# Regrouping transfers on two queues and a later third pair of scores in a fused attention and MLP kernel on one Trainium2 core

## The chip, the cores and the metric

The kernel runs on one core of a Trainium2 chip. The metric is the device time of one execution in microseconds; lower is better. All times here are of one core.

## The reference

What is computed is a layer norm, then multi-query attention (one key and value head for 16 query heads) and an MLP on the normed input, and the sum of all three:

```python
B, S, D, H = 1, 2048, 448, 16          # Dh = 28, F = 1792
def _A_ref(x, wq, wk, wv, wo):
    q = (x @ wq).reshape(B, S, H, Dh).transpose(0, 2, 1, 3)
    k = x @ wk
    v = x @ wv
    scores = jnp.einsum("bhqd,bkd->bhqk", q, k) * (Dh ** -0.5)
    p = _softmax(scores, axis=-1)
    o = jnp.einsum("bhqk,bkd->bhqd", p, v)
    return o.transpose(0, 2, 1, 3).reshape(B, S, H * Dh) @ wo
def _B_ref(x, w1, b1, w2, b2):
    y = _layernorm(x, axis=-1)
    h = _gelu(jnp.einsum("bsd,df->bsf", y, w1) + b1)
    return jnp.einsum("bsf,fd->bsd", h, w2) + b2
xn = _layernorm(x, axis=-1)
return x + _A_ref(xn, A_wq, A_wk, A_wv, A_wo) + _B_ref(xn, B_w1, B_b1, B_w2, B_b2)
```

All data is float32.

## The kernel before

The order of all instructions on each engine is written out by hand; the framework adds the semaphores. The program has three stages: norm and projections (to about 120 us), the MLP with part of the row maxima of the scores beside it (to about 490 us), and attention, in which the change lies.

**Units and steps.** The 2048 queries are cut into 4 chunks of 512, the 16 heads into 4 groups of 4; a unit `u` is one chunk and one group, 16 units in all. The 2048 keys are 16 tiles of 128, and a step treats two key tiles of one unit, so a unit has 8 steps (`kt` = 0, 2, ... 14), and there are 128 steps. The loop at the end of `block_kernel` walks through a string of letters for each step, `ORDERS[0]` for units 0 and 1 and `ORDERS[1]` for units 2 to 15 (`TURNED`), and each letter issues one piece of work:

- `p`: `scores`, a pair of matmuls (L776) that make two heads' or tiles' scores in one of two PSUM buffers, keys in partitions, and one exponential of both on ScalarE (L778). In units 2 to 15 only three of the four heads are made this way, so a step has three pairs.
- `t`, `x`, `T`: the fourth head of units 2 to 15. Its scores are made with queries in partitions (`turned_scores`, `t`, L735), VectorE scales them into a tile `raw` in SBUF and takes the row maximum (L736); four `t` fill one tile of 128 queries, and a unit has four such tiles. `turned_exp` (`x`) makes the exponential of half a tile on ScalarE (L753) and issues eight transfers from SBUF to SBUF (L756), each of 32 partitions by 512 numbers, 64 KB, that regroup the 32-row blocks into the tile `turned` of the unit. `turn_blocks` (`T`) then transposes 32 by 32 blocks of `turned` on VectorE (L761), for two key tiles at a time, so that the keys lie in partitions as for the other heads. The first `T` of a unit needs all 64 transfers of the unit. The work for unit `u` runs ahead, during the unit before; `x` takes one waiting half tile each time, and a second one in the step `kt` = 12. There are three `raw` and two `turned` buffers.
- `P`: the burst, `BURST` = 2 times `pv`: eight matmuls (L715) that multiply the exponentials of the step before with the values and add to the unit's sum `po`. The profile counts 16 matmuls, two passes each.
- `m`: one matmul (L475) and one reduction (L476) of the row maxima for later units, if the plan (`weight`) is behind.
- `e`: `load_max`, once a unit, turns the maxima on TensorE (L458) and sends them into the `q` tile of the next unit.
- `n`: one piece of `norm_jobs`, which divides a finished unit's sum by its softmax denominator; it issues the small transfers `rc`, `ld`, `tr` (L656 to L664) and runs three operations on GpSimd (L667 to L674).
- `o`: one piece of the output projection: for one tile of 128 queries twelve matmuls (L629 to L631), an addition, a transfer to the result.

PSUM banks for `t`, `m`, `e` and `o` come from a pool of three (`mtile`). In the attention stage all loads of `q` (`load_q`, `load_m`) are issued by GpSimd, the 64 transfers a unit of `turned_exp` by SyncE. Each engine and each queue works in the order of its program.

**Output weights.** They are loaded into one of the two `turned` buffers and split there into a high and a low part by `prep_wo`: ScalarE copies (L612) and GpSimd subtracts (L613), four groups, all in step 12.

Of the kernel before, what the change touches and what calls it, by code (L numbers as in the profile page):

```python
# [10 lines left out]
AF = mybir.ActivationFunctionType  # L11
# [7 lines left out]
CT = 4  # L19
NCH = NT // CT  # L20
CW = CT * P
NG = H // 4
# [2 lines left out]
SCALE = DH ** -0.5  # L25
BURST = 2
MLP_MAX = 20
ORDERS = ("mptmpmtmpmexnPTpmonm", "tptmpmeopxnPTmnm")
TURNED = tuple(range(2, 16))
RAWS = 3  # L30
LEAD = 11
# [5 lines left out]
def block_kernel(ctx, tc, x, wq, wk, wv, wo, w1, b1, w2, b2, out):  # L37
    nc = tc.nc
    pe, act, dve, pool = nc.tensor, nc.scalar, nc.vector, nc.gpsimd
    ctx.enter_context(tc.manual_schedule())  # L40

    def f(t):
        return t.bitcast(F32)
# [50 lines left out]
    def mtile(shape):  # L94
        return mp.tile(shape, F32, name="m")
# [95 lines left out]
    def bn_end(c, k0=0, n=CT):  # L191
        for k in range(k0, k0 + n):
            dve.bn_aggr(lnp[:, CT * c + k, :], sts[c][:, k, :])
        ts = slice(CT * c + k0, CT * c + k0 + n)
        r = rstd(lnr[:, ts], lnp[:, ts, 1], n)
        next(r)
        yield
        next(r)
        dve.scalar_tensor_tensor(lnb[:, ts], lnp[:, ts, 0], -1.0, lnr[:, ts], op0=ALU.mult, op1=ALU.mult)
        yield  # L200
# [9 lines left out]
    def norm_both():  # L210
        dve.tensor_mul(lnq, lnp[:, :, 1], lnr)
        dve.tensor_mul(lnq, lnq, lnr)
        r = rstd(lnq, lnq, NT)
        next(r)
        yield
        next(r)
        dve.tensor_mul(lnq, lnq, lnr)
        dve.scalar_tensor_tensor(lnqb, lnp[:, :, 0], -1.0, lnq, op0=ALU.mult, op1=ALU.mult)
        act.activation(warm, one, AF.Gelu_apprx_tanh)
        yield  # L220
# [54 lines left out]
    def norm_gen(c, bank):  # L275
        center, turn = norm_parts(c, True, False, bank)
        for k in range(CT + 1):
            if k < CT:
                center(k)
            if k > 0:  # L280
                turn(k - 1)
            yield
# [88 lines left out]
    for c, at in ((2, ((0, 1), (0, 2), (0, 2), (0, 3))), (3, ((1, 0), (1, 1), (1, 2), (1, 3)))):  # L371
        for k in range(CT):
            later(*at[k], lambda t=CT * c + k: bn(t))
        g = bn_end(c)
        for k in range(2):
            later(c - 1, 0, lambda g=g: next(g), True)
    g = norm_both()
# [28 lines left out]
    for c in range(NCH):  # L406
        center, turn = norm_parts((c + 1) % NCH, c + 1 == NCH)
        for i in range(4):
# [7 lines left out]
            if i in ((2, 3) if c == 0 else (1, 3)):  # L416
                n = 2 * c + i // 3
# [19 lines left out]
    def load_q(u):  # L437
        c, g = units[u]
        cols = slice(c * CW, (c + 1) * CW)
        if u < 2:  # L440
            qst.append(xt_p.tile([P, 4, CW], F32R, name="xh"))
            pool.memset(f(qst[u]), 0.0)
        qs = qst[u % 2]
        for blk, i in ((1, 0), (2, 0), (0, 1), (3, 1)):
            nh = heads_of(u)
            src = qd[i][4 * DH * g:4 * DH * g + DH * nh, cols].rearrange("(j r) n -> r j n", r=DH)
            loads.dma_start(f(qs[32 * blk:32 * blk + DH, 0:nh, :]), src)
        qss[u] = qs
# [50 lines left out]
    mxs, side, oside = Stream(), Stream(), Stream()  # L499
# [63 lines left out]
    for c in range(1, NCH):  # L563
        g = norm_gen(c, lambda shape: php.tile(shape, F32, name="ph"))
# [4 lines left out]
    for n in range(len(mslots) + 2):  # L569
        c, ft = mslots[n] if n < len(mslots) else (NCH, n - len(mslots))  # L570
        if ft == 12:
            for k in range(CT):
                a = acc[:, CT * c + k, :]
# [20 lines left out]
    def turned_tile():  # L594
        return att.tile([P, 4 * CT, CW], F32, name="turned", bufs=2)

    wor = turned_tile()[:, 0:NG, 0:D]
# [5 lines left out]
    woh = att.tile([P, NG, D], F32R, name="woh", bufs=1)  # L603
    wol = att.tile([P, NG, D], F32R, name="wol", bufs=1)
# [2 lines left out]
        src = wo.rearrange("(g j d) n -> j d g n", j=4, d=DH)[j]  # L607
        nc.sync.dma_start(wor[32 * j + 1:32 * j + 1 + DH, :, :], src)

    def prep_wo():  # L610
        for g in range(NG):
            act.activation(woh[:, g, :], wor[:, g, :], AF.Copy)  # L612
            pool.tensor_sub(wol[:, g, :], wor[:, g, :], f(woh[:, g, :]))  # L613

    rows = {}

    def load_rows_of(c, tiles):
        for k in tiles:
            rows[c, k] = att.tile([P, D], F32, name="a", bufs=5)
            loads.dma_start(rows[c, k], ad[:, CT * c + k, :])  # L620

    def o_jobs(c, gs, tiles=range(CT)):
        last = NG - 1 in gs
        for k in tiles:
            po = mtile([P, D])
            ts = slice(k * P, (k + 1) * P)
            for g in gs:
                oth, otl = ots[c, g]
                pe.matmul(po, oth[:, ts], woh[:, g, :], start=(g == gs[0]), stop=False)  # L629
                pe.matmul(po, oth[:, ts], wol[:, g, :], start=False, stop=False)  # L630
                pe.matmul(po, otl[:, ts], woh[:, g, :], start=False, stop=(g == gs[-1]))  # L631
            a = rows[c, k]
            dve.tensor_add(a, a, po)
            if last:
                (nc.scalar if k % 2 and c == NCH - 1 else nc.sync).dma_start(ov[:, CT * c + k, :], a)
            yield
# [73 lines left out]
    def pv(u, kt):  # L710
        if kt == 0:
            pos[u] = op.tile([P, CW], F32, name="po")
        po = pos[u]
        for j in range(4):
            pe.matmul(po[32 * j:32 * j + 32, :], vs[:, kt, :], ps.pop((u, kt, j)),  # L715
                      start=(kt == 0), stop=(kt == NT - 1))
        if kt == NT - 1:
            if u == NU - 1:
                end_jobs(u, pos.pop(u))
                return  # L720
            side.add(norm_jobs(u, pos.pop(u)))
            side.step()
            c, g = units[u]
            if c < NCH - 1 and g == NG - 1:
                oside.add(o_wait(c, range(NG), range(CT if c < NCH - 2 else 2)))

    turned, exps = {}, []

# [17 lines left out]
    def turned_exp():  # L746
        if not exps:
            return
        u, t, raw, m3, h = exps.pop(0)
        if u not in turned:  # L750
            turned[u] = turned_tile()
        rs = slice(2 * h, 2 * h + 2)
        act.activation(raw[:, rs], raw[:, rs], AF.Exp, bias=m3[:, 4:5], scale=1.0)  # L753
        for r in range(2 * h, 2 * h + 2):
            for a in range(4):
                nc.sync.dma_start(turned[u][32 * r:32 * r + 32, 4 * t + a, :],  # L756
                                  raw[32 * a:32 * a + 32, r].rearrange("p b i -> p (b i)"))

    def turn_blocks(u, kt):
        p = pair_of()  # L760
# [11 lines left out]
    def scores(u, kt, jobs):  # L772
        s = sp.tile([P, 2, CW], F32, name="s")
        p = pair_of()
        for i, (k, j) in enumerate(jobs):
            pe.matmul(s[:, i], ks[:, (kt + k) * P:(kt + k + 1) * P], qss[u][:, j, :], start=True, stop=True)  # L776
            ps[u, kt + k, j] = p[:, i]
        act.activation(p, s, AF.Exp, scale=SCALE)  # L778

    def o_wait(c, gs, tiles):  # L780
        load_rows_of(c, tiles)
        for _ in range(8):
            yield
        yield from o_jobs(c, gs, tiles)

    steps = [(u, kt) for u in range(NU) for kt in range(0, NT, 2)]
# [2 lines left out]
    left = total - maxed  # L789
    weight = [0 if n >= len(steps) - LEAD else 24 if u == 0 else 20 if u == 1 else 6 for n, (u, kt) in enumerate(steps)]  # L790
    for n, (u, kt) in enumerate(steps):
        if n == 12:
            prep_wo()
        if u + 1 < NU and kt == 0:
            load_q(u + 1)
        jobs = [((0, 0), (0, 1)), ((0, 2), (1, 2)), ((1, 0), (1, 1))]
        if u not in TURNED:
            jobs[1:2] = [((0, 2), (0, 3)), ((1, 2), (1, 3))]
        for what in ORDERS[u in TURNED]:
            if what == "p":  # L800
                scores(u, kt, jobs.pop(0))
            elif what == "m":
                if maxed < total - left + left * sum(weight[:n + 1]) / sum(weight):
                    maxed += mxs.step()
            elif what == "t":
                if n >= 8 * (TURNED[0] - 1) - 2:
                    tq.step()
            elif what == "x":
                turned_exp()
                if kt == 12:  # L810
                    turned_exp()
            elif what == "T":
                if u in TURNED:
                    turn_blocks(u, kt)
            elif what == "e":
                if kt == (6 if u + 2 < NU else 10) and u + 1 < NU:
                    load_max(u + 1)
            elif what == "n":
                side.step()
            elif what == "o":  # L820
                if n == len(steps) - LEAD:
                    load_rows_of(NCH - 2, (2, 3))
                    for k in (2, 3):
                        for gs in ((0, 1), (2, 3)):
                            oside.add(o_jobs(NCH - 2, gs, [k]))
                elif n == len(steps) - 5:
                    oside.add(o_jobs(NCH - 1, range(NG - 1)))
                if n == len(steps) - 7:
                    load_rows_of(NCH - 1, range(CT))
                oside.step()  # L830
            elif what == "P":
                for _ in range(BURST if n else 0):
                    pv(*pvq.pop(0))
    while pvq:
        pv(*pvq.pop(0))
# [27 lines left out]
```

## Time and profile before

| | us |
|---|---|
| median of 3 runs | 1213.79 (1213.04 to 1216.76) |
| profiled execution | 1212.41 |
| its span on the core | 1210.4 |
| TensorE busy | 1137.7 |
| VectorE busy | 907.4 |
| ScalarE busy | 660.8 |
| GpSimd busy | 353.6 |

The profile is of one execution. The busy times are shares of the span: an engine that is 94% busy over the whole can still wait in one stage, and matmuls are pipelined, so that a busy TensorE is not one at its peak. Instructions that only issue a transfer are not counted as busy on SyncE; the time that SyncE's queue spends on them is read from the order of time. In the rows, PE is TensorE (PEld its weight loads), DVE VectorE, ACT ScalarE, POOL GpSimd, SP SyncE, "SPq" its queue; `out<-in` names the tiles; `L715` is line 715 of the kernel; "idle before <-releaser" is how long the engine stood still ahead of an instruction and what ended it. In the chain and the timeline the first number is the start in us from the span's start, the second the duration.

### The profile page before, as it was taken

How to read it: one execution, taken by the hardware profiler on the slowest of the kernel's cores; microseconds unless marked ns; L12 is line 12 of the kernel's file. 1: busy time of each engine (PE TensorE's matmuls, PEld its weight loads, DVE VectorE, ACT ScalarE, POOL GpSimd, SP SyncE). 2: the span in 40 equal slices, each digit the busy share in tenths (PEclk: the TensorE clock that was granted, in tenths of full speed). 3: DMA queues.
4: the chain of work that ended last, by engine and by line, in shares of the span. 5: the costliest groups of instructions: out<-in, count | busy, mean ns of one | idle time of the engine just before them, and what ended most of it. 6: DMA issues, size and time to landing. Idle time of an engine off the chain costs nothing.

```text
span 1210.4 us, 17322 instructions
## 1 busy us (share of the span) xinstructions
PE 1137.7 (94%) x5793; PEld 722.4 (60%) x5793; DVE 907.4 (75%) x1678; ACT 660.8 (55%) x778; POOL 353.6 (29%) x473
## 2 busy tenths in 40 slices
PE   9999999999999999899989889989889989889998
PEld 8778888888888888544434345334345434344444
DVE  7799999999999999677767566667656767657634
ACT  5842321221221112578877666777766768668763
POOL 5333331131122123525243332143232233223310
PEclk9999999999999999999999899999989989899999
DMA  8651101001000120424554654554654555555520
GB/s 282 198 166 52 35 20 54 16 24 46 24 16 23 47 54 17 119 62 107 126 142 120 156 146 127 123 144 123 161 137 120 132 135 132 132 131 132 130 86 31
DMA packets 77733, 121.86 MB, mean 101 GB/s; under 512 B 24862, under 2 KB 33756, under 8 KB 77516
## 3 DMA queue, kind: packets, MB, share of 16 engines
q1 hardware_dynamic: 64204, 95.63, 29.2%
q0 software_dynamic: 12032, 24.55, 8.1%
q8 instruction: 46, 0.75, 0.3%
q10 hardware_dynamic: 1408, 0.57, 0.2%
q14 instruction: 43, 0.35, 0.1%
HBM read 46.11 MB, written 14.79 MB: 50 GB/s over the span
## 4 chain that ended last, share of the span: by engine, by line
PE 74%; DVE 7%; ACT 7%; DMA 6%; SPq 3%; issue 2%; POOL 0%; ACTq 0%; DVEq 0%; POOLq 0%
PE po L715 16%; PE m L475 14%; PE s L776 12%; PE ph L159 9%; ACT p L778 6%; DMA turned<-raw 5%; PE m L735 4%; PE m L532 3%; PE m L534 3%; PE m L530 3%; SPq L756 3%; DVE mx L476 2%; PE qp L159 2%; DVE p L761 2%; PE m L629 1%
## 5 line engine op out<-in xcount | busy, mean ns | idle before, releaser
L476 DVE TENSOR_REDUCE mx<-m 128x1 f32<-128x512 f32 x800 | 521.4, 686 | 52.1 <-PE m L475 46.8
L778 ACT ACTIVATE p<-s 128x1024 f32<-128x1024 f32 x400 | 387.7, 1022 | 202.0 <-PE s L776 188.8
L475 PE MATMUL m<-ks,qm 128*128 128x512 f32 x800 | 320.5, 404 | 42.4 <-DVE raw L736 41.1
L776 PE MATMUL s<-xh,ks 128*128 128x512 f32 x800 | 265.9, 416 | 19.2 <-ACT p L778 17.8
L761 DVE STREAM_TRANSPOSE p<-turned 128x1024 f32<-128x1024 f32 x112 | 139.4, 1245 | 170.5 <-ACT p L778 72.7
L715 PE MATMUL po<-p,vs 128*32 128x512 f32 x2048 | 258.1, 618 | 1.1 <-DVE p L761 1.1
L516 ACT ACTIVATE hr<-ph,b1t 128x512 f32<-128x512 f32 x56 | 38.6, 688 | 305.4 <-PE ph L164 299.5
L475 PEld LDWEIGHTS m<-ks,qm 128*128 128x128 f32 x800 | 151.6, 190 | 84.1 <-DVE raw L736 46.3
L776 PEld LDWEIGHTS s<-xh,ks 128*128 128x128 f32 x800 | 143.0, 191 | 98.4 <-ACT p L778 64.8
L521 POOL TENSOR_TENSOR hl<-hr,hh 128x512 fp32r<-128x512 f32 x56 | 72.1, 1288 | 301.7 <-PE m L475 284.6
L736 DVE TENSOR_SCALAR_CACHE_REDUCE raw<-m 128x512 f32<-128x512 f32 x224 | 149.6, 684 | 8.7 <-PE m L735 4.3
L715 PEld LDWEIGHTS po<-p,vs 128*32 128x32 f32 x2048 | 55.1, 111 | 133.1 <-issue 129.3
L753 ACT ACTIVATE raw<-raw,m 128x1024 f32<-128x1024 f32 x112 | 127.6, 1139 | 0.0
L735 PE MATMUL m<-ks,q 128*128 128x512 f32 x224 | 99.6, 445 | 0.0
L735 PEld LDWEIGHTS m<-ks,q 128*128 128x128 f32 x224 | 42.1, 188 | 94.5 <-issue 80.1
L530 PE MATMUL m<-w2h,hh 128*128 128x448 f32 x224 | 82.4, 368 | 0.0
L534 PE MATMUL m<-w2h,hl 128*128 128x448 f32 x224 | 81.9, 366 | 0.0
L532 PE MATMUL m<-w2l,hh 128*128 128x448 f32 x224 | 81.8, 365 | 0.0
L159 PE MATMUL ph<-xh,w1l 128*128 128x512 f32 x168 | 66.3, 394 | 0.0
L159 PE MATMUL ph<-xl,w1h 128*128 128x512 f32 x168 | 66.1, 394 | 0.0
L159 PE MATMUL ph<-xh,w1h 128*128 128x512 f32 x168 | 66.0, 393 | 0.0
L462 POOL DMA_DIRECT2D xh<-mn x15 | 8.0, 535 | 193.8 <-ACT mn L460 193.8
(148 smaller groups left out, 1124.6 us busy)
## 6 DMA issues: line engine op xcount, KB each, us to landing
turned<-raw SPq DMA_DIRECT2D x896, 64.0 KB
xh<-qd POOLq DMA_DIRECT2D x56, 168.0 KB, 5.1
qm<-qd SPq DMA_DIRECT2D x148, 56.0 KB
qd<-qe SPq DMA_DIRECT2D x24, 256.0 KB
ad<-acc SPq DMA_DIRECT2D x4, 896.0 KB
tr<-ld POOLq DMA_DIRECT2D x56, 64.0 KB, 2.5
a<-ad POOLq DMA_DIRECT2D x16, 224.0 KB, 4.1
raw<-in_B_w_dram SPq DMA_DIRECT2D x7, 448.0 KB
```

The source lines that it names most:

```text
L159: pe.matmul(ps, w, v, start=(n == 0), stop=False)
L475: pe.matmul(pm, qm[:, t * P:(t + 1) * P], ks[:, n * CW:(n + 1) * CW], start=True, stop=True)
L476: dve.tensor_reduce(mx[:, CT * j + t, n:n + 1], pm, axis=AX.X, op=ALU.max)
L530: pe.matmul(m2[k], hh[:, ts], w2h[:, ft, :], start=(ft == 0), stop=False)
L534: pe.matmul(m2[k], hl[:, ts], w2h[:, ft, :], start=False, stop=(ft == NF - 1))
L715: pe.matmul(po[32 * j:32 * j + 32, :], vs[:, kt, :], ps.pop((u, kt, j)), start=(kt == 0), stop=(kt == NT - 1))
L735: pe.matmul(sc, q3[i][:, t * P:(t + 1) * P], ks[:, n * CW:(n + 1) * CW], start=True, stop=True)
L736: dve.tensor_scalar(raw[:, :, 4 * n:4 * n + 4, :].rearrange("p r b i -> p b r i"), sc.rearrange("p (b r i) -> p b r i", r=4, i=32), SCALE, ...
L753: act.activation(raw[:, rs], raw[:, rs], AF.Exp, bias=m3[:, 4:5], scale=1.0)
L761: dve.transpose(p.rearrange("p k (g j) -> p g k j", j=32), turned[u][:, :, 32 * kt:32 * kt + 64].rearrange("p g (k j) -> p g k j", j=32))
L776: pe.matmul(s[:, i], ks[:, (kt + k) * P:(kt + k + 1) * P], qss[u][:, j, :], start=True, stop=True)
L778: act.activation(p, s, AF.Exp, scale=SCALE)
```

## The change

Four places change; the third is a consequence for the output rows of chunk 2.

- In `turned_exp`, GpSimd issues three of the eight transfers of a half tile (those with `a` = 3, and `a` = 2 where `r` is odd), SyncE the other five.
- In `ORDERS[1]` the third `p` of a step moves behind the burst `P`, the second `t` moves behind `T`, and `o` moves ahead of `x`; the three `p` of a step are now two ahead of `P` and one behind it. In `ORDERS[0]` the letter `T`, which did nothing there, goes.
- The output projection of chunk 2 (`NCH - 2`) is queued whole, four tiles, when its last unit ends; before, two tiles were, and the other two came in halves from step 117 on.
- `prep_wo` takes one group and is called in steps 2, 3, 4 and 5 instead of all four groups in step 12.

```diff
-ORDERS = ("mptmpmtmpmexnPTpmonm", "tptmpmeopxnPTmnm")
+ORDERS = ("mptmpmtmpmexnPpmonm", "ptpmeoxnPpTtmmnm")
...
-    def prep_wo():
-        for g in range(NG):
-            act.activation(woh[:, g, :], wor[:, g, :], AF.Copy)
-            pool.tensor_sub(wol[:, g, :], wor[:, g, :], f(woh[:, g, :]))
+    def prep_wo(g):
+        act.activation(woh[:, g, :], wor[:, g, :], AF.Copy)
+        pool.tensor_sub(wol[:, g, :], wor[:, g, :], f(woh[:, g, :]))
...
-                oside.add(o_wait(c, range(NG), range(CT if c < NCH - 2 else 2)))
+                oside.add(o_wait(c, range(NG), range(CT)))
...
-                nc.sync.dma_start(turned[u][32 * r:32 * r + 32, 4 * t + a, :],
-                                  raw[32 * a:32 * a + 32, r].rearrange("p b i -> p (b i)"))
+                q = pool if a == 3 or (a == 2 and r % 2) else nc.sync
+                q.dma_start(turned[u][32 * r:32 * r + 32, 4 * t + a, :],
+                            raw[32 * a:32 * a + 32, r].rearrange("p b i -> p (b i)"))
...
-        if n == 12:
-            prep_wo()
+        if 2 <= n < 2 + NG:
+            prep_wo(n - 2)
...
-                if n == len(steps) - LEAD:
-                    load_rows_of(NCH - 2, (2, 3))
-                    for k in (2, 3):
-                        for gs in ((0, 1), (2, 3)):
-                            oside.add(o_jobs(NCH - 2, gs, [k]))
-                elif n == len(steps) - 5:
+                if n == len(steps) - 5:
                     oside.add(o_jobs(NCH - 1, range(NG - 1)))
```

## The prediction

> **What bounds the kernel now.** First the page: engine shares and the chain of work that ended last. Then the list of waits, the chain in order of time, and the order of instructions in one step.
>
> ```profile
> PE 1137.7 (94%) x5793; PEld 722.4 (60%) x5793; DVE 907.4 (75%) x1678; ACT 660.8 (55%) x778; POOL 353.6 (29%) x473
> ...
> PE 74%; DVE 7%; ACT 7%; DMA 6%; SPq 3%; issue 2%; POOL 0%; ACTq 0%; DVEq 0%; POOLq 0%
> ```
> ```profile
> DVE p L761 <- DMA turned<-raw: 61.4, 11, 7.3
> POOL oc L667 <- DMA tr<-ld: 30.4, 13, 3.3
> POOL tr L664 <- DMA ld<-rc: 27.7, 14, 3.5
> ```
>
> TensorE looks full, but the chain holds two foreign pieces, DMA and SyncE's queue. The waits name the transfer: in 11 places VectorE's transposition in `turn_blocks` ("the turn", L761) stands 5.6 us on average for `turned<-raw`. The chain in order of time, in which L715 is the burst of eight `po` matmuls that each step holds once, tells what that does to a step:
>
> ```profile
> 589.40 1.85 PE po L715 x16
> 594.07 1.85 PE po L715 x16
> ...
> 626.65 1.90 PE po L715 x16
> ...
> 629.24 4.37 DMA turned<-raw
> ...
> 637.14 2.58 PE po L715 x16
> ```
> ```profile
> 1138.85 1.50 PE L715 MATMUL po<-p,vs 128*32 128x512 f32 x12
> ```
>
> An ordinary step takes 594.07 - 589.40 = 4.67 us. The step that enters a new unit takes 637.14 - 626.65 = 10.49, 5.8 more: the turn waits, VectorE empties no PSUM bank behind it, TensorE stands, and the next burst itself takes 2.58 instead of 1.85. I number the steps by n: the burst of n=16 is at 589.40, that of n=116 at 1138.85 (timeline). These 100 steps take 549.5 us; at 4.66 each they would take 466. So 83.5 us are something else: waits at its 12 unit changes (n=24, 32, ... 112), and the output projections.
>
> Why the transfers are late is read from SyncE's queue and from the windows:
>
> ```profile
> 643.51 24.53 SPq L756 DMA_DIRECT2D turned<-raw  x38
> ```
> ```profile
> 589.40:1144.20 554.80, 500.77 (x2718) 239.19 (x2721) 368.21 (x746) 404.60 (x432) 166.84 (x270) 0.95 0.53 134
> 849.82:858.84 9.02, 5.33 (x28) 2.48 (x27) 3.44 (x8) 4.60 (x6) 2.94 (x5) 0.90 0.91 229
> ```
>
> SyncE issues without a pause, 24.53/38 = 0.646 us per transfer. A step makes eight: 5.17 us of issuing in a step of 4.66. The queue loses 0.5 us a step, 4 us a unit, and the next unit's first turn collects the debt. The DMA engines are 0.53 busy over the stage (column before the last), 0.91 in a stretch with a stall and GpSimd's loads in it: not full on average, close to it for moments.
>
> **Part 1, three of eight transfers on GpSimd.** SyncE keeps five: 5 x 0.646 = 3.2 us a step, under 4.66. Its debt is gone. GpSimd gets three:
>
> ```profile
> L399 POOL DMA_DIRECT2D qm<-qd x52 | 26.4, 514 | 49.6 <-PE m L475 46.5 <-DMA xh<-qd 2.6 <-DMA qm<-qd 0.6
> L447 POOL DMA_DIRECT2D xh<-qd x60 | 36.9, 619 | 58.9 <-PE s L776 48.2 <-PE m L735 9.9 <-PE m L475 0.5
> L674 POOL TENSOR_TENSOR otl<-oc,oth 128x512 fp32r<-128x512 f32 x15 | 19.3, 1288 | 4.3 <-ACT oth L671 3.1
> ```
> ```profile
> xh<-qd POOLq DMA_DIRECT2D x56, 168.0 KB, 5.1
> ```
> ```profile
> 1119.92 2.20 DMA turned<-raw
> ```
> ```profile
> 733.40 1.25 DVE L761 STREAM_TRANSPOSE p<-turned 128x1024 f32<-128x1024 f32 x1 [0.91 <-ACT p L778]
> ```
>
> No row shows this transfer issued by GpSimd. The nearest, `qm<-qd` (56 KB beside 64), takes 0.51; the larger `xh<-qd` 0.62. I take 0.51. A unit's 24 cost 12.3 us; GpSimd is now busy 166.84 us in 554.8, that is 13.2 in a unit of 44, and waits in its order for `ld` and `tr` to land, (30.4+27.7)/14 = 4.2. Together 29.7 of a unit's 37.3: it fits. Queued behind the new transfers are the loads of `q`, the output's `rc`, `ld`, `tr` and the split L667 to L674; all are needed a unit later. The other way round, the new transfers stand behind `ld`, `tr` and the 1.29-us products.
>
> The deadline. With the second `t` now behind `x`, a tile's first exponential comes a step later, and the fourth tile's two are made together in the seventh step of a unit (before: seventh and, for the first half, sixth). From the end of the first, SyncE has ten issues, 6.5 us, and the last lands 2.20 later (row above): 8.7. The next unit's first turn is due two steps on, about 8.6 after it: two steps of 4.66, plus 0.3 for the second exponential, plus 1.2 by which the turn trails its burst (733.40, with the burst at 732.23, below), less 2.2 by which the exponential's end trails its own (850.85 + 1.14 against 849.82, below). So the last piece comes just in time. It can be 2.2 late: landing took 4.37 in the chain above, and `load_q`, whose pieces need 5.1, is issued in the step between. I take 0.6 us of wait a unit, between 0 and 2.5.
>
> Here the Trainium skill speaks against the change: "DMA: Bandwidth & Descriptors", section "Issuing engines are not separate DMA queues", says that transfers from all queues run on the same 16 engines and that several issuers save only the issue time, usually small. The share of 0.53 and the even 0.646 us say that issue time is what is short here; by the rule taken strictly the stalls would stay (a rival below).
>
> **Part 2, the third pair behind the burst.** One step before:
>
> ```profile
> 847.02 0.50 PE L735 MATMUL m<-ks,q 128*128 128x512 f32 x1
> 847.36 0.63 PE L776 MATMUL s<-xh,ks 128*128 128x512 f32 x2
> ...
> 848.06 0.39 PE L475 MATMUL m<-ks,qm 128*128 128x512 f32 x1
> 848.28 0.62 PE L776 MATMUL s<-xh,ks 128*128 128x512 f32 x2
> 849.16 0.73 PE L776 MATMUL s<-xh,ks 128*128 128x512 f32 x2 [0.26 <-ACT p L778]
> 849.82 1.92 PE L715 MATMUL po<-p,vs 128*32 128x512 f32 x16
> 851.68 0.51 PE L735 MATMUL m<-ks,q 128*128 128x512 f32 x1
> ```
> ```profile
> 848.08 2.87 ACT L778 ACTIVATE p<-s 128x1024 f32<-128x1024 f32 x3 [0.75 <-PE s L776]
> 850.85 1.14 ACT L753 ACTIVATE raw<-raw,m 128x1024 f32<-128x1024 f32 x1
> ```
>
> The loop of 4.66: burst to first `t` 1.86 (851.68 - 849.82), `t` to first pair 0.34, first pair to third pair 1.80 (two PSUM buffers: the third waits for the first's exponential), third pair to burst 0.66. In the new order p t p m P p t m the pair that waits is the second (for the exponential of the pair behind the last burst). The loop is: burst to third pair 1.86, third pair to the next second pair 1.80 plus 0.1 (a pair's second matmul comes 0.1 later right behind the burst, as `t` to pair 0.34 against 0.23 for 848.28 - 848.06), second pair to burst 0.66 + 0.22 for the `m` that now lies in between. Sum 4.64: `t` leaves the loop, `m` enters it, nothing is won. ScalarE has 2.87 + 1.14 = 4.0 in it, VectorE (368.21 of 554.80 us) about 3.1, the rest of TensorE fits in the 1.9: no other engine takes over. I keep 4.66, between 4.43 (`m` finds cover) and 4.8.
>
> Three things lose cover because they lie after the second pair, on the loop:
>
> ```profile
> 729.22 0.38 PE L629 MATMUL m<-woh,oth 128*128 128x448 f32 x1
> ...
> 731.68 0.63 PE L776 MATMUL s<-xh,ks 128*128 128x512 f32 x2
> 732.23 1.92 PE L715 MATMUL po<-p,vs 128*32 128x512 f32 x16
> ```
>
> An output tile's twelve matmuls take 731.68 - 729.22 = 2.46, now whole. Chunk 2's last two tiles join the others, so 12 such steps lie in the stretch: 29.5 us. The transposition of the maxima is at most one matmul's 0.22, 13 times: 2.9. The doubled exponential (1.14 more on ScalarE, of which the 0.75 idle above takes most) makes the next pair's 0.3 late, 12 times: 3.6.
>
> **Part 3, output weights in steps 2 to 5.**
>
> ```profile
> 505.99 3.85 ACT L778 ACTIVATE p<-s 128x1024 f32<-128x1024 f32 x4 [1.73 <-PE s L776]
> 561.89 1.96 ACT L612 ACTIVATE woh<-turned 128x448 fp32r<-128x448 f32 x4
> ```
>
> Now ScalarE does four copies in a row, 1.96 us ahead of a step's pairs. One copy is 0.49, and in those early steps ScalarE stands 1.73 us just there. Gain: 0 to 1.96, I take 1.2. If the weights have not landed by then, the cover is gone and a first step pays a few us.
>
> **Tail.** The half tiles that chunk 2 had in steps 117 to 120 go, the last chunk's nine matmuls lose cover four times:
>
> ```profile
> 1170.21 1.85 PE po L715 x16
> ...
> 1191.25 1.85 PE po L715 x16
> 1195.67 4.31 PE po L715 x32
> ```
>
> Four steps of (1191.25 - 1170.21)/4 = 5.26 become 4.42 + 9 x 0.205 = 6.27 (4.42 = 1195.67 - 1191.25, no `o` and no `t`). The seven others from 1138.85 on come to 31.3 at 4.42 plus 0.3. Together 56.4 against 56.8: -0.4.
>
> **Sum.** New stretch: 100 x 4.66 = 466, + 29.5 + 2.9 + 3.6 + 12 x 0.6 = 7.2, in all 509.2 against 549.5: -40.3. With -1.2 and -0.4: -41.9. The profiled execution took 1212.4 us (span 1210.4 and 2.0 around it), 1.4 under the median of the runs. 1212.4 - 41.9 = **1170.5**. A difference of 0.3% (3.6 us) is about what a measurement can tell from none.
>
> **Rivals.**
> - *Late pieces stay late* (0.18): GpSimd's six last pieces behind `tr`, product and `q` loads, or the crowding of `load_q`, cost 2.5 us a unit. For it: 0.91 busy in the stall window, landings of 4 to 5 us. Against: two steps of room. 1170.5 + 12 x 1.9 = 1193.
> - *The step itself gets shorter* (0.11): the `m` behind the second pair finds room and the loop is 4.43. 1170.5 - 100 x 0.23 = 1148.
> - *GpSimd becomes the queue that is too slow* (0.06), the slower side. Its other work is 17.4 us a unit; over 44 us, today's mean unit (8 x 5.495), it decides: each of 24 transfers would have to cost over 1.1 us. Against: 0.51 and 0.62. At 1.3 a unit takes 48.6, 4.6 more in each of 12.5 (100 steps): about 1270.
> - *The DMA engines are the limit* (0.04): the transfers go no faster from two queues; the stalls stay and swallow the lost cover. 1212, no change.
>
> The forecast has 0.61, its own range 1157 to 1190. The range of 8 in 10 takes in the two rivals beside it, without their far ends: 1146 to 1203. Faster by over 0.3%: 0.61 + 0.18 + 0.11 and a little of the last, 0.90; within: 0.03; slower: 0.07.
>
> **What would show it.** Right: SyncE's `turned<-raw` no longer back to back; "turn waits for DMA turned<-raw" from 61 us to under 10; steps inside a unit still 4.6 to 4.7 us; steps with `o` near 7.1; the clock column 1.00 through the stage; GpSimd about 0.2 fuller. Wrong: unit changes that still take 9 us, with GpSimd's transfers issued last; steps over 4.8 or under 4.5; GpSimd transfers over 0.7 us.

## The result, and the profile after

The changed kernel takes 1159.19 us (median of 4 runs, 1156.78 to 1161.25) against 1214.22 for the kernel before beside it: a ratio of 0.9543, 95% interval 0.9518 to 0.9569. The forecast was 1170.5, the range 1146 to 1203. The execution in the profile took 1156.78 us, 55.6 less than the one before, where 41.9 were forecast.

The page of the changed kernel, its engine shares, clock and chain:

```profile
PE 1119.7 (97%) x5793; PEld 712.7 (62%) x5793; DVE 914.1 (79%) x1676; ACT 661.1 (57%) x778; POOL 518.9 (45%) x809
...
PEclk9999999999999999989999999999999999999999
...
PE 67%; ACT 11%; DMA 6%; DVE 6%; issue 3%; POOL 3%; SPq 2%; ACTq 0%; DVEq 0%; POOLq 0%
...
L756 POOL DMA_DIRECT2D turned<-raw x336 | 167.7, 506 | 130.3 <-ACT raw L752 120.6
```

TensorE is busy for 18.0 us less, and its share is up because the span is shorter by more. GpSimd's transfers take 0.506 us, as assumed. The line of the waits that answers to the first one of before, and a window of the stage (columns: start and end, length, busy time and count of PE, PEld, DVE, ACT and POOL, granted clock, DMA share, GB/s):

```profile
DVE p L761 <- DMA turned<-raw: 3.9, 5, 1.4
```
```profile
590.00:1090.00 500.00, 487.33 (x2746) 234.46 (x2750) 377.09 (x749) 405.85 (x432) 313.73 (x569) 1.00 0.58 151
```

The turn waited 61.4 us for the pieces before, now 3.9. These rows hold only the waits that the profile puts down to the pieces; all idle time of VectorE ahead of the first turns of the twelve units from n=24 to n=112 sums to 66.5 us before and 10.7 now. TensorE is 97% busy inside the stage (before 500.77 of 554.80, 90%), at a granted clock of 1.00 where it was 0.95. The DMA engines are only a little fuller (0.58, before 0.53). A step in the order of time, and its counterpart in the chain:

```profile
641.79 1.92 PE L714 MATMUL po<-p,vs 128*32 128x512 f32 x16
643.64 0.73 PE L776 MATMUL s<-xh,ks 128*128 128x512 f32 x2
644.21 0.40 PE L734 MATMUL m<-ks,q 128*128 128x512 f32 x1
644.45 0.39 PE L475 MATMUL m<-ks,qm 128*128 128x512 f32 x1
644.67 0.63 PE L776 MATMUL s<-xh,ks 128*128 128x512 f32 x2
645.14 0.40 PE L734 MATMUL m<-ks,q 128*128 128x512 f32 x1
645.50 0.73 PE L776 MATMUL s<-xh,ks 128*128 128x512 f32 x2
646.06 0.39 PE L475 MATMUL m<-ks,qm 128*128 128x512 f32 x1
646.38 1.92 PE L714 MATMUL po<-p,vs 128*32 128x512 f32 x16
```
```profile
709.30 1.85 PE po L714 x16
716.34 1.85 PE po L714 x16
```

The step takes 646.38 - 641.79 = 4.59 us and the loop is the one forecast: burst to third pair 1.85 (1.86), third to second pair 1.86 (1.90), second pair to burst 0.88 (0.88). A step with an output tile takes 716.34 - 709.30 = 7.04. Two points on the order of the letters: `o` stood ahead of `x` before too, and loses its cover because the third `p` no longer stands between it and the burst; and one of the two `m` ahead of the burst went behind it as well.

What decides at a unit change is seen on SyncE, ScalarE and VectorE around the changed kernel's step n=32 (three views in the order of time):

```profile
657.57 6.21 SPq L756 DMA_DIRECT2D turned<-raw  x10
```
```profile
656.39 2.19 ACT raw L752 x2
```
```profile
661.61 1.25 DVE L761 STREAM_TRANSPOSE p<-turned 128x1024 f32<-128x1024 f32 x1 [0.37 <-PE po L714]
666.24 1.25 DVE L761 STREAM_TRANSPOSE p<-turned 128x1024 f32<-128x1024 f32 x1
```

The unit's last two exponentials begin at 656.39; SyncE's ten issues end at 663.78; the next unit's first turn is due, and starts, at 666.24 with no wait. That is 9.85 us after the exponentials begin, with 2.5 us left for the landing. It is just enough, and experiments 3 and 4 show how little is to spare.

### The profile page after: what moved, and what is told of

Same layout as the page of the kernel before. It is cut to its first block, busy times and chain, and to the rows that moved or that the text cites. A ratio compares the mean times of both kernels' runs of the same rounds, so it can differ in the third digit from the quotient of the medians.

```text
span 1155.0 us, 17693 instructions
## 1 busy us (share of the span) xinstructions
PE 1119.7 (97%) x5793; PEld 712.7 (62%) x5793; DVE 914.1 (79%) x1676; ACT 661.1 (57%) x778; POOL 518.9 (45%) x809
## 4 chain that ended last, share of the span: by engine, by line
PE 67%; ACT 11%; DMA 6%; DVE 6%; issue 3%; POOL 3%; SPq 2%; ACTq 0%; DVEq 0%; POOLq 0%
PE m L475 14%; PE po L714 13%; PE s L776 11%; PE ph L159 9%; ACT p L778 6%; PE m L532 4%; PE m L534 4%; PE m L530 4%; ACT raw L752 3%; DMA turned<-raw 3%; DVE mx L476 2%; SPq L756 2%; POOL turned L756 2%; PE m L734 2%; PE m L628 1%
## 5 line engine op out<-in xcount | busy, mean ns | idle before, releaser
L476 DVE TENSOR_REDUCE mx<-m 128x1 f32<-128x512 f32 x800 | 526.7, 688 | 77.4 <-PE m L475 71.7
L475 PE MATMUL m<-ks,qm 128*128 128x512 f32 x800 | 317.1, 400 | 1.4 <-DVE mx L476 0.6
L776 PE MATMUL s<-xh,ks 128*128 128x512 f32 x800 | 277.5, 430 | 25.6 <-ACT p L778 24.8
L776 PEld LDWEIGHTS s<-xh,ks 128*128 128x128 f32 x800 | 131.3, 189 | 198.5 <-ACT p L778 94.9
L714 PE MATMUL po<-p,vs 128*32 128x512 f32 x2048 | 246.5, 598 | 0.1
L756 POOL DMA_DIRECT2D turned<-raw x336 | 167.7, 506 | 130.3 <-ACT raw L752 120.6
L735 DVE TENSOR_SCALAR_CACHE_REDUCE raw<-m 128x512 f32<-128x512 f32 x224 | 153.0, 685 | 45.8 <-PE m L734 42.1
L761 DVE STREAM_TRANSPOSE p<-turned 128x1024 f32<-128x1024 f32 x112 | 139.2, 1243 | 48.8 <-PE po L714 21.7
L734 PE MATMUL m<-ks,q 128*128 128x512 f32 x224 | 88.9, 397 | 0.0
```

What stands on the lines that cost most here:

```text
L475: pe.matmul(pm, qm[:, t * P:(t + 1) * P], ks[:, n * CW:(n + 1) * CW], start=True, stop=True)
L476: dve.tensor_reduce(mx[:, CT * j + t, n:n + 1], pm, axis=AX.X, op=ALU.max)
L734: pe.matmul(sc, q3[i][:, t * P:(t + 1) * P], ks[:, n * CW:(n + 1) * CW], start=True, stop=True)
L735: dve.tensor_scalar(raw[:, :, 4 * n:4 * n + 4, :].rearrange("p r b i -> p b r i"), sc.rearrange("p (b r i) -> p b r i", r=4, i=32), SCALE, ...
L756: q.dma_start(turned[u][32 * r:32 * r + 32, 4 * t + a, :], raw[32 * a:32 * a + 32, r].rearrange("p b i -> p (b i)"))
L761: dve.transpose(p.rearrange("p k (g j) -> p g k j", j=32), turned[u][:, :, 32 * kt:32 * kt + 64].rearrange("p g (k j) -> p g k j", j=32))
```

## The experiments

All medians are set against runs of the kernel before on the same chip in the same job (1213.97 to 1214.40).

**1. The split alone, and the change without it.** Do the queue, or the order and the weights, carry the gain? `split_only` is the kernel before with this edit, `no_split` the changed kernel without it:

```diff
-                nc.sync.dma_start(turned[u][32 * r:32 * r + 32, 4 * t + a, :], ...
+                q = pool if a == 3 or (a == 2 and r % 2) else nc.sync
+                q.dma_start(turned[u][32 * r:32 * r + 32, 4 * t + a, :], ...
```

> The kernel before with the split of the eight transfers alone (three on GpSimd); order, output rows and weights as before. Theory A (SyncE's issue time of 0.646 us per transfer made the stalls): the waits at the unit changes go, inside a unit the step stays at 4.66, output tiles keep their cover of 1.92 us: the 100 steps take about 466 + 20, the kernel about 1151 (1143 to 1160), no slower than the changed kernel. Rival B (the new order of scores brought the gain): over 1195. Rival C (the DMA engines are the limit): 1214.

Measured: 1156.86 (1155.14 to 1157.59), ratio 0.9521 [0.9496, 0.9546], within the expected range.

> The changed kernel with all eight transfers back on SyncE. Theory A: SyncE is short again (5.17 us of issuing in a step of 4.60), and the last tile's sixteen transfers are now issued together, so the unit changes stall as before or longer: 1214 to 1240. Rival B (the order brought the gain): near 1160.

Measured: 1264.79, ratio 1.0416 [1.0383, 1.0448], beyond the expected end. Its waits, and SyncE's queue:

```profile
DVE p L760 <- DMA turned<-raw: 114.7, 13, 12.7
```
```profile
639.88 22.64 SPq L755 DMA_DIRECT2D turned<-raw  x33
```

The three transfers on GpSimd carry the whole gain. The two versions that have the split lie within 2.3 us of each other and their intervals overlap, so the order, the output rows and the earlier weights together bring nothing that these runs can tell. With SyncE alone the new order is 50 us worse than the old one: it makes a unit's last exponential in one step with the one before, and the wait of the turn goes from 61.4 to 114.7 us.

SyncE's debt itself can be read where the last half tile of a unit is issued (the kernel before at n=24, then `split_only` at n=32; ScalarE and SyncE's queue):

```profile
618.30 1.14 ACT L753 ACTIVATE raw<-raw,m 128x1024 f32<-128x1024 f32 x1
623.70 5.04 SPq L756 DMA_DIRECT2D turned<-raw  x8
```
```profile
655.61 1.14 ACT L753 ACTIVATE raw<-raw,m 128x1024 f32<-128x1024 f32 x1
656.77 3.04 SPq L757 DMA_DIRECT2D turned<-raw  x5
```

Before, the exponential ends at 619.44 and its eight issues begin 4.3 us later, behind those of the half tiles ahead of them; at the unit's first half tile it was 0.1. In `split_only` SyncE's five begin at once.

The equal medians hide two differences. In the profiled executions `split_only` is ahead of the change by 4.7 us when the burst of n=116 begins (1079.70 against 1084.41; 1.4 of it up to n=16, 3.3 in the 100 steps) and then loses 5.5, mostly in one step of 12.46 us at n=118. There VectorE's addition of an output tile stands for rows of chunk 2:

```profile
1093.42 0.62 DVE L633 TENSOR_TENSOR a<-a,m 128x448 f32<-128x448 f32 x1 [8.43 <-DMA a<-ad]
```

GpSimd issues that load only at 1090.53, after the transfers, a product and the small loads ahead of it in its order. In the kernel before the same addition waits 4.05 us; the changed kernel, which queues these rows otherwise, does not wait there. So in these two executions the new order and the early weights cost a little, and the other queueing of the output rows makes up for it.

**2. Is it the issuing or the moving?** `half_bytes` is the kernel before; each transfer moves half of its numbers, as many transfers as before.

```diff
+            pool.memset(turned[u][:, :, 256:512], 1.0)
...
-                nc.sync.dma_start(turned[u][32 * r:32 * r + 32, 4 * t + a, :], raw[...])
+                nc.sync.dma_start(turned[u][32 * r:32 * r + 32, 4 * t + a, 0:256], raw[...][:, 0:256])
```

> The kernel before with as many transfers on SyncE, each of half the bytes (256 of 512 columns; the other half of the tile is filled with ones by GpSimd, so a part of the regrouping is left out). Theory A: the issue time per transfer stays at 0.6 to 0.65, the stalls stay, 1205 to 1220. Rival C (bytes and DMA engines are the limit): the stalls shrink to under 2 us a unit, about 1160 to 1175.

Measured: 1202.41, ratio 0.9898 [0.9860, 0.9936], 2.6 us under the expected range. SyncE's queue, the waits, and 100 us of the stage (columns as above):

```profile
639.76 22.49 SPq L757 DMA_DIRECT2D turned<-raw  x34
```
```profile
DVE p L762 <- DMA turned<-raw: 50.4, 7, 9.9
```
```profile
600.00:700.00 100.00, 89.07 (x492) 40.15 (x488) 68.92 (x142) 75.78 (x82) 44.07 (x64) 0.95 0.35 92
```

The DMA share falls to 0.35 (0.56 in the same 100 us of the kernel before), and an issue still costs 22.49/34 = 0.661 us. The stalls stay: 50.4 us of waits, 61.4 before. It is the issuing on one queue that counts here, not the bytes. Each transfer has its 32 rows in both kernels, so this run does not tell a cost of the issue from a cost of its rows. The fill has waits of its own on GpSimd, so the 12 us that were won are not a clean price of the bytes.

**3. The dose.** One and two of eight on GpSimd instead of three, in the changed kernel:

```diff
-                q = pool if a == 3 or (a == 2 and r % 2) else nc.sync
+                q = pool if a == 3 and r % 2 else nc.sync     # one_of_eight
+                q = pool if a == 3 else nc.sync               # two_of_eight
```

> The changed kernel with one of the eight transfers on GpSimd instead of three. Theory A: SyncE issues 7 x 0.646 = 4.5 us in a step of 4.6, so its debt is just gone, but the last two half tiles need 14 issues, 9.0 us, and 2.2 to land, where 8.6 to 9 are to be had: about 2 us of wait a unit, 1159 + 12 x 2 = 1183 (1172 to 1195). Rival C (the queues share the DMA engines, how they are divided does not matter): as with none, 1265, or as with three, 1159.

Measured: 1229.71, ratio 1.0130 [1.0094, 1.0166].

> The changed kernel with two of the eight transfers on GpSimd. Theory A: twelve last issues, 7.8 us, and 2.2 to land: about 0.6 us a unit, 1159 + 8 = 1167 (1158 to 1172).

Measured: 1184.97, ratio 0.9761 [0.9726, 0.9796]. Both are slower than expected: 0, 1, 2, 3 of 8 give 1265, 1230, 1185, 1159. The time follows how the transfers are divided, so rival C is out. By the mean rate six issues of 0.634 us in a step of 4.60 leave SyncE time to spare. It has that time, and its pieces are late all the same. The run with two of eight at its first unit change (SyncE's queue, ScalarE and VectorE in the order of time), and the same turn in the run with one of eight:

```profile
623.59 7.48 SPq L756 DMA_DIRECT2D turned<-raw  x12
```
```profile
622.41 2.19 ACT L752 ACTIVATE raw<-raw,m 128x1024 f32<-128x1024 f32 x2
635.43 1.25 DVE L761 STREAM_TRANSPOSE p<-turned 128x1024 f32<-128x1024 f32 x1 [3.38 <-DMA turned<-raw]
```
```profile
635.61 1.25 DVE L761 STREAM_TRANSPOSE p<-turned 128x1024 f32<-128x1024 f32 x1 [5.96 <-DMA turned<-raw]
```

The exponentials begin at 622.41, the twelfth issue ends at 631.07, and the last piece lands about 4.4 us later; the turn was due at 635.43 - 3.38 = 632.05. This is the deadline of the prediction's part 1. Both expectations had it, with 2.2 us for the landing; the last pieces took about twice that here. Why they land later than in the row with 2.20 stays open.

**4. The deadline by itself.** `last_half` keeps the mean low and relieves only the last row tile of a unit (the one whose two exponentials come together): four of its eight on GpSimd, one of eight elsewhere.

```diff
-                q = pool if a == 3 or (a == 2 and r % 2) else nc.sync
+                q = pool if a == 3 and (r % 2 or t == CT - 1) or a == 2 and t == CT - 1 else nc.sync
```

> Edit: the changed kernel, but GpSimd issues 4 of the 8 transfers of a unit's last two exponentials (its fourth row tile) and 1 of 8 of the other six, 14 of a unit's 64 in all; 24 of 64 in the change, 16 in the run with 2 of 8, 8 in the run with 1 of 8. Theory D (a deadline): the last two exponentials of a unit are issued in one step, and the next unit's first transposition, due 9.6 us after the first of them begins (657.4-1.0 to 666.24 in the changed kernel), needs all their pieces; with n of 16 on SyncE the last issue comes about 1.2 + 0.634n us after it and lands 3 to 4.5 us later: 10 of 16 are just in time, 12 are 3 us late, 8 are in time. In ordinary steps 7 x 0.634 = 4.44 us stays under the step's 4.60. So the stalls at unit changes go, and the time is that of the change, about 1160 (1155 to 1168), though GpSimd has fewer transfers than in the run with 2 of 8 (1185). Rival R (the mean rate or the share of GpSimd decides): between the runs with 1 and 2 of 8, about 1185 + 44.7 x 2/8 = 1196 (1188 to 1210).

Measured: 1168.53 (1163.60 to 1170.52), ratio 0.9625 [0.9605, 0.9646].

```profile
DVE p L761 <- DMA turned<-raw: 8.4, 3, 3.8
ACT woh L611 <- DMA turned<-in_A_wo_dram: 3.8, 1, 3.8
```
```profile
632.14 1.25 DVE L761 STREAM_TRANSPOSE p<-turned 128x1024 f32<-128x1024 f32 x1 [0.20 <-PE po L714]
```

With 14 of a unit's 64 transfers on GpSimd it is 16 us faster than the run with 16 of 64 in even shares; the median is half a microsecond over the end of the deadline's range and 20 under the rival's. Eleven of the twelve unit changes between n=16 and n=116 are ordinary steps. One, at an output tile, takes 10.94 us where the change has 7.04. So the deadline carries most of the dose. Against the change the profiled execution's span is 6.8 us longer: 3.1 up to n=16, where the first copy of the weights waits 3.8 us (the change: 1.1), and 3.9 in that one step. The edit does not touch the early part: that wait differs from kernel to kernel with the same early steps (the first step takes 7.26 us in the change, 10.58 here, 10.37 in the run of `m_late` below).

**5. The weights in steps 8 to 11.** In the change the weights' split cost time where it was forecast to gain. The edit to the changed kernel:

```diff
-        if 2 <= n < 2 + NG:
-            prep_wo(n - 2)
+        if 8 <= n < 8 + NG:
+            prep_wo(n - 8)
```

First the steps of the change on ScalarE (order of time):

```profile
503.25 0.58 ACT L611 ACTIVATE woh<-turned 128x448 fp32r<-128x448 f32 x1 [1.13 <-DMA turned<-in_A_wo_dram]
503.73 2.85 ACT L778 ACTIVATE p<-s 128x1024 f32<-128x1024 f32 x3
508.37 1.03 ACT L778 ACTIVATE p<-s 128x1024 f32<-128x1024 f32 x1 [1.78 <-PE s L776]
509.29 0.56 ACT L611 ACTIVATE woh<-turned 128x448 fp32r<-128x448 f32 x1
509.75 2.86 ACT L778 ACTIVATE p<-s 128x1024 f32<-128x1024 f32 x3
```

The idle 1.78 us lies ahead of a step's fourth exponential, during the burst; the copy stands behind that exponential, ahead of the next step's three. It has no cover, and the first copy waits for the weights' DMA as well.

> The changed kernel with the output weights split in steps 8 to 11 instead of 2 to 5. Theory E (the copies stand on ScalarE ahead of a step's first pair and not in its idle time, and the first of them waits for the weights to land): steps 2 to 5 go back from 7.3, 6.1, 6.0, 6.0 to 5.6, and steps 8 to 11, where VectorE is the bound, stay at 6.0 to 6.3: 3 us less, 1156. Rival: the copies cost the same wherever they are: 1159.

Measured: 1154.10 (1151.18 to 1154.69), ratio 0.9503 [0.9479, 0.9527]. Steps 2 to 5 are back at 5.58, 5.71, 5.57 and 5.58 us (in the change 7.26, 6.14, 6.03, 6.02), and P(16), the burst of n=16, begins at 586.78 instead of 590.79. Of these 4.0 us 3.0 lie in steps 2 to 5; the other 1.0 lies ahead of the first burst, whose start differs by up to 2.8 us between the traces of these kernels. By the medians the gain is 5.1, with overlapping intervals.

**6. A tighter step.** Between the third pair and the next second pair TensorE has time; `m_late` moves the `m` between the second pair and the burst of the changed kernel there, off the loop:

```diff
-ORDERS = ("mptmpmtmpmexnPpmonm", "ptpmeoxnPpTtmmnm")
+ORDERS = ("mptmpmtmpmexnPpmonm", "ptpeoxnPpTtmmmnm")
```

> The changed kernel with the maxima's matmul between the second pair and the burst moved behind the burst. Theory D (a step is the loop burst, third pair, its exponential, second pair, burst): the loop loses one matmul, 4.60 becomes 4.38, 1159 - 100 x 0.22 = 1137 (1132 to 1143). Rival (the step is bounded by the sum of TensorE's work, or by the three PSUM banks): 1155 to 1163.

Measured: 1153.21 (1152.06 to 1155.58), ratio 0.9495 [0.9469, 0.9521]: 6 of the 22 us expected. Most steps inside a unit are 4.37 to 4.48 us with one `m` and 4.50 with two. One with two:

```profile
642.96 1.92 PE L714 MATMUL po<-p,vs 128*32 128x512 f32 x16
644.81 0.73 PE L776 MATMUL s<-xh,ks 128*128 128x512 f32 x2
645.38 0.40 PE L734 MATMUL m<-ks,q 128*128 128x512 f32 x1
645.61 0.63 PE L475 MATMUL m<-ks,qm 128*128 128x512 f32 x2
646.08 0.63 PE L776 MATMUL s<-xh,ks 128*128 128x512 f32 x2
646.57 0.50 PE L734 MATMUL m<-ks,q 128*128 128x512 f32 x1
646.91 0.63 PE L776 MATMUL s<-xh,ks 128*128 128x512 f32 x2
647.47 1.92 PE L714 MATMUL po<-p,vs 128*32 128x512 f32 x16
```

The matmuls follow each other without a gap: the time that was free is used up by the moved `m`, and TensorE's own work sets this step. A step with one `m` and 4.37 us is what the theory expected. Up to n=16 this run takes 2.6 us more than the change, as the first copy of the weights waits longer.

`m_o_late_prep_8` moves the output tile too, behind the burst, and has the weights in steps 8 to 11 (the edit of 5):

```diff
-ORDERS = ("mptmpmtmpmexnPpmonm", "ptpmeoxnPpTtmmnm")
+ORDERS = ("mptmpmtmpmexnPpmonm", "ptpexnPpoTtmmmnm")
```

> The changed kernel with the maxima's matmuls and the output tiles moved behind the burst and the third pair, and the weights split in steps 8 to 11. From the kernel with late maxima (1153): the weights no longer hold step 2 (5 us), and an output tile's 2.46 us get back a cover of 0.3 to 0.5 in each of 16 steps: 1153 - 5 - 6 = 1142 (1138 to 1148). Rival (the window behind the third pair is already full of TensorE's work): 1148.

Measured: 1166.55, ratio 0.9605 [0.9578, 0.9632]: wrong, 7 us slower than the change. VectorE in the order of time:

```profile
707.06 0.62 DVE L632 TENSOR_TENSOR a<-a,m 128x448 f32<-128x448 f32 x1 [4.01 <-PE m L630]
707.75 1.25 DVE L761 STREAM_TRANSPOSE p<-turned 128x1024 f32<-128x1024 f32 x1
```
```profile
677.20 0.25 DVE L658 RECIPROCAL rc<-rc 128x16 f32<-128x16 f32 x1 [4.81 <-DMA rc<-oc]
```

The addition of the output tile now stands ahead of the turn in VectorE's order, and waits 4.01 us for matmuls that come after the burst; four such steps take 6.63 + 8.78 + 7.70 + 8.37 = 31.5 (the change: 28.3). And in three units the reciprocal of `norm_jobs` waits for its transfer (13.3 us in all, 4.8 the longest), with everything behind it on VectorE; in the change it waits nowhere. Why that transfer took up to 8.6 us to land (6.0 in the change) stays open.

The last run puts the two edits that helped together, and leaves the output tile where the change has it:

> Edit: the changed kernel with the two max tiles of a step moved between the third pair and the next second pair (the output tile stays where it is) and the weights split in steps 8 to 11. Theory: the two gains add. The maxima late gave 1159.2 - 1153.2 = 6 although its early stage lost about 4 us to a first copy that waited 3.5 us for the weights; the split in steps 8 to 11 gave 5.1 and takes that wait away: 1153.2 - 5.1 - 1 = 1147 (1143 to 1151), with steps of 4.37 to 4.51, output steps of 6.9 to 7.1 and no stall at unit changes. Rival: shorter steps alone bring the stalls of the run in which the output tile was late too (the reciprocal's DMA and the pieces then come after their due time): 1155 to 1167, with steps over 8 us near unit changes.

Measured: **1146.75** (1145.42 to 1148.19), ratio 0.9441 [0.9424, 0.9458], as expected by the sum. It beats both kernels: its interval lies below that of the change. Against the run above only the place of the output tile differs: 19.8 us. But the theory expected no stall at unit changes, and some are left: three output steps there take 7.67, 8.33 and 8.39 us where the change has 7.04, 7.26 and 7.04, two steps right behind a unit change take 5.43 and 4.73 for 4.50, and the idle time ahead of the twelve first turns is 21.7 us (the change: 10.7). The two steps over 8 us are the rival's sign; the whole costs about 4 us. What ends each of these waits stays open.

```profile
PE 1113.6 (97%) x5793; PEld 711.6 (62%) x5793; DVE 904.1 (79%) x1676; ACT 661.3 (58%) x778; POOL 520.5 (45%) x809
```

## Why the prediction was right, point by point

P(16) and P(116) are the starts of those bursts: 589.40 and 1138.85 before, 590.79 and 1084.40 after. So the time to n=16 is 1.4 us longer, the stretch of 100 steps takes 493.6 against 549.45, 55.8 less, and the rest from P(116) to the end of the execution is 1.2 shorter: together -55.6.

- *Part 1, the queue: right in kind, shown.* SyncE's issue time was the limit; split alone, all of the gain; half the bytes, the stalls stay; fewer transfers moved, a smaller gain. The rival by which the DMA engines are the limit is out, for this kernel. The Trainium skill's "DMA: Bandwidth & Descriptors", section "Issuing engines are not separate DMA queues", says that issuing from several engines saves only the issue time, usually small beside the transfer itself. The traces agree with the first half: the debt of issue time went, and halving the bytes saved only 1%. An issue of 0.65 us is indeed shorter than the 2.20 us of a landing, but with eight of them in a step of 4.66 us it was not small: moving three to GpSimd saved 4.8%.
- *The wait at unit changes: mis-sized.* Forecast 12 x 0.6 = 7.2, measured almost none: of the twelve steps at unit changes only that of n=72 is longer than its like, 7.26 for 7.04. The margin is real but thin: two more of sixteen issues on SyncE (12 for 10) and unit changes stall. "Late pieces stay late" did not cost 2.5 us a unit, but its order of events is in the trace: at n=24 GpSimd issues the unit's last three pieces from 627.20 on, 5.7 us after their exponential has ended, and the turn waits 1.4 us, until 0.3 us after they have landed. In the run with two of eight pieces were late in earnest, and mostly SyncE's.
- *Part 2, the step: right to 0.06.* Forecast 4.66, measured 4.60; third to second pair took 1.86, 0.06 of the 0.1 added, and the sum of 4.64 had been rounded up to 4.66. Over 100 steps 6 us, the second largest part of the miss. The rival of 4.43 did not come by this order; moving the `m` off the loop brought 4.37 to 4.50.
- *The small terms.* Output steps 7.04, 2.44 over an ordinary one (forecast 2.46); the doubled exponential 4.87, 0.28 (0.3); the transposed maxima 4.70, 0.10 (0.22). With the two terms above: 7.2 + 6 + about 2 = 15 of the 15.6 us by which the stretch came out shorter than 509.2.
- *Part 3, the weights: wrong.* Forecast -1.2, measured +1.4 up to n=16. Taking the copies out of step 12 gained 1.4 us (7.42 to 6.04), as forecast. What was put at nothing is their cost in steps 2 to 5: 25.45 us against 22.46, 3.0 more. The failed step is "ScalarE stands 1.73 us just there". The row of four exponentials with the 1.73 ahead of it begins with one step's fourth exponential, behind the burst; the other three belong to the next step, and the copy stands between the two, where ScalarE does not wait. The other condition, that the weights "have not landed by then", came true as well, for 1.1 us of the first copy. With the copies in steps 8 to 11 P(16) comes 589.40 - 586.78 = 2.6 us earlier than before; 0.7 of it is the step from P(15) to P(16), where the new order begins (5.33 to 4.65).
- *Tail: right.* -0.4 forecast, -0.9 measured to n=127 (55.9 for the 56.4; output steps 6.18 for 6.27); the other 0.3 lie behind it.
- *What would show it.* SyncE's queue has pauses, the turn waits 3.9 us (under 10), the steps are 4.59 to 4.60 (the band's lower end), output steps near 7.1, the clock 1.00: as forecast. GpSimd is fuller by 313.73/500 - 166.84/554.8 = 0.33 in the stage, not 0.2: 24 transfers of 0.506 in a unit of 37 us are that much by themselves.

What stays argued only: that the new order is no gain by itself rests on medians 2.3 us apart and on the stages of one profiled execution each, and its parts were not run one by one.

## What to carry to other kernels

Look at the queue that issues, not only at the engines that move: a queue without a pause, with a constant time for each issue whatever the bytes, is a bound that the engine shares don't show, and a second issuer removes it. Then look for the deadline and not the mean rate: the group of transfers that is issued last and needed first sets how many must move, and relieving that group alone brought most of the gain. Before moving an instruction into "idle" time, see on which side of its neighbours the idle time lies, and what is queued behind it on every engine that touches its result.

## What the runs showed of the hardware

- A transfer's issue on SyncE costs the same at 64 KB and at 32 KB (0.646 and 0.661 us); GpSimd's issue of the same 64 KB costs 0.506, and lands 2.4 us after it begins at the median, 7.8 at most.
- In these runs TensorE is slower for a while after a long stall. In the run of experiment 4, in a first step of 10.58 us, TensorE stands 4.05 us for an exponential, and the burst behind that takes 3.59 us instead of 1.92 at a granted clock of 0.57 (TensorE in the order of time, and the window 507 to 511 us). So the stall costs more than its own length. In the changed kernel's stage the granted clock stays at 1.00.

```profile
505.48 1.22 PE L776 MATMUL s<-xh,ks 128*128 128x512 f32 x2 [4.05 <-ACT p L778]
507.06 3.59 PE L714 MATMUL po<-p,vs 128*32 128x512 f32 x16
```
```profile
507.00:511.00 4.00, 4.00 (x19) 0.97 (x19) 0.69 (x1) 0.77 (x1) 1.51 (x3) 0.57 0.32 90
```
